# A spectral filter beside a routed expert layer on one core: the forward 32-point step of four pairs of groups on float16 halves, the last tile in column halves with some output transfers on ScalarE's queue, and a new order of the work

## The chip, the cores and the metric

One Trainium2 chip, one core. The core has a matrix engine (TensorE, PE in the profile), VectorE (DVE), ScalarE (ACT), GpSimd (POOL) and SyncE (SP), which issues the transfers; 16 DMA engines move the data. PE writes to PSUM, eight banks of 2 KB per partition; VectorE and ScalarE read it from there. The metric is device microseconds of one execution, the median over runs.

## The reference

Input `x` is 2048 by 576 (rows n, columns d). The result is the sum of two branches, each fed with the layer norm of `x`, and of `x` itself.

```python
X = rfft2(LN(x));  y_A = irfft2(X * (w_r + 1j * w_i), s=(2048, 576))      # spectral filter

q = einsum("nd,dhc->nhc", LN(x), w_q)          # 32 heads, c = 2 x 128
s1 = q[..., :128] @ k1.T;  s2 = q[..., 128:] @ k2.T      # 8 scores each
# top 1 of s1 and of s2 per head -> one of 64 experts; weights by softmax over K = 1
y_B = sum over heads of gelu(LN(x) . u[expert]) * v[expert]               # routed experts

out = x + y_A + y_B
```

The two-dimensional transform is written as matrix products: over d (576 points, folded by symmetry into even and odd halves) and over n (2048 = 64 x 32 points, with the filter's weights between the forward and the inverse half).

## The kernel before

**Forward, first half.** `x` lies in SBUF as 16 tiles of 128 rows (`XN`). Five loads bring it, of 2, 2, 4, 4 and 4 tiles (`LOADS`). For each tile `ln` finds mean and variance (on VectorE, for tiles 7, 9, 11, 13, 15 on ScalarE), `folds` makes sums and differences of mirrored columns (tiles `t` for the first fold, `F` in the tag `A2` for the second; `DF` lists the tiles whose odd part is folded on VectorE, the others go to GpSimd), ScalarE makes `Rs` (a 128-by-128 float32 matrix scaled by the rows' inverse deviations) and `yl` (three copies of the 33 columns left over), and `dft128` multiplies them on PE and stores the result in `AB` and `ABL`.

**The weights of the scores.** `fold_part` reads `w_q` once, in 32 transfers of 576 KB into five buffers `w`, and multiplies each with `KP` (the differences of the keys). `fold_end` and `fold_last` turn and scale the result (`MT`) into `MU` and `MUL`, in float16 high and low parts. With that the layer norm, the queries and the keys are one product of `x` with `MU`.

**The 16 groups of frequencies.** For a group g, `d_fwd(g)` is the step over d (PE, from `ABL` and `AB`, 6 matmuls; ScalarE copies the PSUM to a float32 tile `A2`). `s_fwd(g)` is the 32-point step of the pair g, g+1: 16 float32 matmuls on quarters of the array (64 by 64), weights `S16`, data `A2`. `s_mul(g)` multiplies by the filter's weights (two VectorE instructions of 578 columns, then GpSimd and ScalarE make `y`, `yh`, `yl`). `s_inv(g)` is the step back over n, 36 float16 matmuls on high and low halves (ScalarE and VectorE store the results in `AB`, `ABL`). `load_w` and `load_s16` fetch the weights ahead.

**The routed experts, r = 0 to 7**, 256 rows each. `x_t(r)` loads the transposed x (`xf`) and splits it into float16 halves (`xT`). `scores(r)` is 28 matmuls `MU,xT` and `MUL,xT` of 128 by 512, followed on VectorE by a reduce to `mx` and two products; `route` and `combine` are more VectorE work, with a few instructions on ScalarE, GpSimd and PE, and end in `CAT`.

**The end.** For tile t, `d_inv(t)` is the step back over d, with VectorE and GpSimd joining the halves; `fin(t)` multiplies the last 64-point step and the experts' part into PSUM (the matmuls `A,c` and `vS,MT`), VectorE adds `x` into `XN` (one instruction of 576 columns), and two transfers of 64 partitions by 288 columns by 2 rows (144 KB) go to the output. All are issued by SP.

**What sets the order.** Nothing is issued where it is written: every operation is recorded in a planner (`_Plan`) with an estimated cost and its dependences; a list scheduler (`forward`) then picks, engine by engine, the ready operation with the smallest number in a table, `RANK`, one number per operation; buffers (tags with 2 to 5 copies, as `w` 5 and `A2` 2 for groups and 4 for folds) and PSUM banks (`LIMIT`) hold operations back. The result is one fixed order per engine, and in it each engine issues strictly in turn. All operations are issued from one helper line, L542 of before, which is why the profile's rows all carry that line and are told apart by the tiles they name.

Of the kernel before, what the change touches and what calls it, by code (L numbers as in the profile page):

```python
# [32 lines left out]
def _consts():  # L33
# [55 lines left out]
    s16 = np.concatenate([(fw * 64).astype(np.float32), np.concatenate(_hl(iv), 2).view(np.float32)], 2)  # L89
# [42 lines left out]

CHANGE = 97.0

RANK = (
# [158 lines left out]
class _Plan:  # L294
# [7 lines left out]
    def cost(self, eng, m, out, ins, kw):  # L302
        n = 1
# [5 lines left out]
        if eng == "tensor":  # L309
# [5 lines left out]
            if kw.get("tile_position"):  # L315
                q = _parts(ins[0])
                return c * q[0] * q[1] / 16384 * (0.935 if q == [64, 128] else 1.065), 230.0
# [243 lines left out]
def _body(ctx, tc, nc, plan, a, out):  # L561
# [580 lines left out]
    def fin(t, y):  # L1142
# [12 lines left out]
        for c in range(2):  # L1155
            Q.dma_start(os[t, c], x[64 * c:64 * c + 64])
# [121 lines left out]
```

## Time and profile before

| what | value |
|---|---|
| median of three runs | 214.45 us (214.44 to 216.28) |
| the profiled execution, its own time | 215.94 us |
| its span, first to last instruction | 214.2 us |
| mean granted clock of TensorE | 0.987 |
| PE busy | 191.7 us (89%), 2324 matmul records |
| VectorE busy | 178.3 us (83%), 426 instructions |
| ScalarE, GpSimd busy | 129.8 us (61%), 112.9 us (53%) |
| moved by DMA | 48.12 MB, 225 GB/s over the span |

The page cuts the span into 40 slices of 5.36 us. In it PE is busy from the third slice to the last but one; VectorE is full at the start and from the nineteenth slice on, with a thinner middle; the DMA engines are full to the nineteenth slice, nearly idle in the stage of the experts, and half busy in the last six slices. A float32 matmul leaves several records in the trace, a float16 one leaves one. Times in the rows are microseconds from the start of the span: start, then duration; in square brackets stands how long the engine had been idle and what ended that.

### The profile page before, as it was taken

The page shows a single profiled execution, that of the slowest core. Times are in us where ns is not written, and L with a number is a line of the kernel's source. Part 1 is how long each engine was busy: PE and PEld are TensorE (multiplying, and loading weights), DVE is VectorE, ACT ScalarE, POOL GpSimd, SP SyncE. Part 2 cuts the span into 40 slices and gives each one's busy share as a digit, 9 for nine tenths or more (in the row PEclk, how much of TensorE's full clock was granted, in tenths as well). Part 3 has the DMA queues.
Part 4 walks back from the last instruction along what each step waited for, and adds up shares of the span by engine and source line. Part 5 has one row for each costly group of instructions (what it writes and reads, how often), then busy time and mean ns, then how long its engine had stood idle before and what let it go on. Part 6 is the DMA issues. An engine that isn't in the chain of part 4 may idle for free.

```text
span 214.2 us, 6027 instructions
## 1 busy us (share of the span) xinstructions
PE 191.7 (89%) x2324; PEld 131.4 (61%) x2324; DVE 178.3 (83%) x426; ACT 129.8 (61%) x304; POOL 112.9 (53%) x153
## 2 busy tenths in 40 slices
PE   0093999989999999999999999999999999999980
PEld 0082877757856765674648464476465777878850
DVE  1999899941694956992999999999999999999880
ACT  2279699888948792984845964996454531222310
POOL 4356464612419840492523663879565147758750
PEclk9999799999999999999999999999999999999998
DMA  6999999999999999998543433102000000655566
GB/s 202 392 413 422 396 312 313 415 409 410 384 384 387 411 410 381 424 411 352 142 123 95 153 112 95 55 3 77 0 5 0 3 0 5 167 139 139 123 161 164
DMA packets 17020, 48.12 MB, mean 225 GB/s; under 512 B 2144, under 2 KB 8544, under 8 KB 16224
## 3 DMA queue, kind: packets, MB, share of 16 engines
q1 hardware_dynamic: 16992, 47.74, 62.7%
q8 instruction: 18, 0.29, 0.6%
q14 instruction: 10, 0.08, 0.1%
HBM read 43.01 MB, written 4.72 MB: 223 GB/s over the span
## 4 chain that ended last, share of the span: by engine, by line
PE 54%; DVE 32%; issue 5%; ACT 2%; POOL 2%; DMA 2%; DVEq 0%; POOLq 0%
PE banks L542 54%; DVE t L542 8%; DVE MT L542 5%; DVE A L542 4%; DVE st L542 3%; DVE w L542 2%; DVE AB L542 2%; DMA XN<-in_x_dram 2%; DVE ABL L542 2%; POOL t L542 2%; DVE mx L542 1%; DVE mm__96 L542 1%; DVE rr L542 1%; ACT yl L542 1%; POOL y L542 1%
## 5 line engine op out<-in xcount | busy, mean ns | idle before, releaser
L542 PE MATMUL banks<-MU,xT 128*128 128x512 f16 x192 | 45.2, 379 | 0.0
L542 PE MATMUL banks<-c,AB 128*128 128x145 f16 (+2 forms) x320 | 37.7, 251 | 0.4 <-DVE AB L542 0.4
L542 PEld LDWEIGHTS <-xT 128*128 128x128 f16 x224 | 20.9, 98 | 23.7 <-issue 0.4
L542 POOL TENSOR_TENSOR y<-t,t 128x289 f32<-128x289 f32 x32 | 23.2, 744 | 21.3 <-DVE t L542 19.1
L542 POOL TENSOR_TENSOR A<-t 128x289 f32<-128x289 f32 (+2 forms) x42 | 26.5, 649 | 14.7 <-PE banks L542 5.6
L542 DVE SCALAR_TENSOR_TENSOR t<-banks,wx,Wt 128x578 f32<-128x578 f32 x32 | 24.4, 811 | 4.4 <-ACT A L542 2.8
L542 POOL TENSOR_TENSOR yh<-y,yh 128x578 f16<-128x578 f32 x16 | 20.8, 1309 | 10.2 <-ACT yh L542 6.8
L542 PE MATMUL banks<-Rs,yl 128*99 128x128 f32 x64 | 11.2, 319 | 15.0 <-ACT yl L542 14.7
L542 POOL TENSOR_TENSOR xT<-xf,xT 128x640 f16<-128x640 f32 x10 | 14.2, 1428 | 17.8 <-ACT xf L542 11.0
L542 ACT ACTIVATE AB<-banks 128x512 f32<-128x512 f32 (+1 forms) x32 | 18.7, 591 | 3.8 <-PE banks L542 3.7
L542 PE MATMUL banks<-w,KP 128*32 128x288 f32 x256 | 20.3, 415 | 0.2 <-DMA w<-in_wq_dram 0.2
L542 ACT ACTIVATE yh<-banks 128x290 f32<-128x290 f32 (+1 forms) x16 | 7.3, 458 | 20.2 <-PE banks L542 13.5
L542 PEld LDWEIGHTS banks<-Rs,yl 128*99 128x99 f32 x64 | 9.0, 195 | 16.7 <-ACT yl L542 15.1
L542 PE MATMUL banks<-c,ABL 99*128 99x289 f16 (+1 forms) x64 | 19.1, 298 | 0.0
L542 POOL TENSOR_TENSOR t<-XN 128x289 f32<-128x289 f32 x14 | 13.1, 942 | 10.9 <-DVE A L542 5.3
L542 PEld LDWEIGHTS banks<-c,AB 128*128 128x128 f32 x128 | 18.0, 190 | 1.3 <-DVE AB L542 0.6
L542 PEld LDWEIGHTS banks<-Rs,A 128*128 128x128 f32 x128 | 16.7, 207 | 3.3 <-issue 2.3
L542 PE MATMUL banks<-Rs,A 128*128 128x128 f32 x128 | 18.3, 295 | 0.0
L542 DVE TENSOR_REDUCE MT<-w 128x128 bf16<-128x896 bf16 (+1 forms) x16 | 18.2, 1138 | 0.0
L542 PE MATMUL banks<-A,s 64*64 64x289 f32 x256 | 17.5, 410 | 0.0
L542 PEld LDWEIGHTS <-AB 128*128 128x128 f16 x192 | 17.2, 147 | 0.1
L542 DVE TENSOR_TENSOR ABL<-banks,ABL 33x256 f16<-33x256 f32 x32 | 13.0, 410 | 5.0 <-ACT ABL L542 4.7
(129 smaller groups left out, 408.4 us busy)
## 6 DMA issues: line engine op xcount, KB each, us to landing
w<-in_wq_dram SPq DMA_DIRECT2D x32, 576.0 KB, 6.9
xf<-in_xT_dram SPq DMA_DIRECT2D x16, 320.0 KB, 5.1
Wt<-in_W_dram SPq DMA_DIRECT2D x8, 578.0 KB, 6.6
out_dram<-XN SPq DMA_DIRECT2D x32, 144.0 KB, 2.5
XN<-in_x_dram SPq DMA_DIRECT2D x3, 1154.0 KB, 9.2
s<-in_s_dram SPq DMA_DIRECT2D x16, 192.0 KB, 4.4
XN<-in_xd_dram SPq DMA_DIRECT2D x2, 1152.0 KB, 9.0
XN<-in_xd_dram SPq DMA_DIRECT2D x1, 2304.0 KB, 10.6
```

The costliest lines, as they stand in the source:

```text
L542: ins = fn(*[x.place() if isinstance(x, _Ps) else x for x in args], **{k: x.place() if isinstance(x, _Ps) else x for k, x in kw.items()}).ins
```

## The change

1. **`s_fwd` on float16 halves** for the groups 0 to 7 (`PAIRS = (0,1,2,3)`). The host gives the forward weights of these groups as high and low float16 halves, in the same bytes. In `d_fwd`, ScalarE writes the high half of `A2` as float16, and a new VectorE instruction subtracts it from the PSUM to make the low half (128 by 578), one for each of the 8 groups. `s_fwd` sums three products (high by high, low weight by high, high weight by low): 48 float16 matmuls for a pair in place of 16 float32 ones.
2. **The first load** of two tiles of `x` becomes two of one tile; `ln` treats these tiles one by one.
3. **`folds`**: in the tiles of `DF` the two VectorE additions of 145 columns become one of 2 by 145.
4. **`fin(15)`** in two column halves (columns 0 to 143 and 144 to 287 of each block): twice the matmuls at half the columns, two VectorE additions of 2 by 144, four transfers of 72 KB. The second transfer (`c` = 1) of tiles 13 and 14 and of both halves of 15 is issued from ScalarE's queue.
5. **The planner's constants** (costs of a few kinds of operation, the price of a change of matmul shape, a cold start of PE, the port that VectorE and GpSimd share) are altered, and `RANK` is new. The order of everything is made anew.

```diff
+PAIRS = (0,1,2,3,)
 RANK = (
-    464, 1220, 901, 1223, 1261, 1268, 1219, 1221, 391, 444, 431, 691, 894, 879, 874, 922, 835, 890, 883, 839,
...
+    1031, 1229, 1032, 1219, 1241, 1243, 1242, 1033, 1245, 730, 572, 810, 562, 803, 319, 320, 329, 377, 707,
...
-    s16 = np.concatenate([(fw * 64).astype(np.float32), np.concatenate(_hl(iv), 2).view(np.float32)], 2)
+    fw = np.stack([np.concatenate(_hl(v), 1).view(np.float32) if g // 2 in PAIRS else v.astype(np.float32) for g, v in enumerate(fw * 64)])
+    s16 = np.concatenate([fw, np.concatenate(_hl(iv), 2).view(np.float32)], 2)
...
-    LOADS = ((0, 2), (2, 2), (4, 4), (8, 4), (12, 4))
-    Q.dma_start(XN[:, 0:2], xs[:, 0:2])
+    LOADS = ((0, 1), (1, 1), (2, 2), (4, 4), (8, 4), (12, 4))
+    Q.dma_start(XN[:, 0:1], xs[:, 0:1])
...
-        (V if t in DF else G).tensor_tensor(F[:, 1, 0:145], e[:, 1, 0:145], e[:, 1, 288:143:-1], op=OP.add)
-        V.tensor_tensor(F[:, 0, 0:145], e[:, 0, 0:145], e[:, 0, 288:143:-1], op=OP.add)
+        if t in DF:
+            V.tensor_tensor(F[:, :, 0:145], e[:, :, 0:145], e[:, :, 288:143:-1], op=OP.add)
+        else:
+            G.tensor_tensor(F[:, 1, 0:145], e[:, 1, 0:145], e[:, 1, 288:143:-1], op=OP.add)
+            V.tensor_tensor(F[:, 0, 0:145], e[:, 0, 0:145], e[:, 0, 288:143:-1], op=OP.add)
...
     def d_fwd(g):
-        A2[g] = T([128, 2, L], F32, "A2", 2)
-        A.activation(A2[g], p[:, :, :L], AF.Copy)
+        if g // 2 in PAIRS:
+            A2[g] = T([128, 2, 2, L], F16, "A2", 2)
+            A.activation(A2[g][:, 0], p[:, :, :L], AF.Copy)
+            V.tensor_tensor(A2[g][:, 1], p[:, :, :L], A2[g][:, 0], op=OP.subtract)
+        else:
+            A2[g] = T([128, 1, 2, L], F32, "A2", 2)
+            A.activation(A2[g][:, 0], p[:, :, :L], AF.Copy)
...
     def s_fwd(g):
+        sf = [(S16[g + q][:, :192].bitcast(F16) if g // 2 in PAIRS else S16[g + q][:, :192]) for q in range(2)]
+        hl = ((0, 0), (0, 1), (1, 0)) if g // 2 in PAIRS else ((0, 0),)
         for m in range(2):
             for b in range(2):
-                w = 64 * (0, 1, 1, 2)[2 * m + b]
...
+                for n, (ha, hb) in enumerate(hl):
+                    w = 64 * (0, 1, 1, 2)[2 * m + b] + 192 * hb
...
+                            P.matmul(ps[q][o:o + 64, m, :L], sf[q][r, w:w + 64], A2[g + q][r, ha, b, :],
+                                     start=(b == n == 0), stop=(b == 1 and n == len(hl) - 1), tile_position=(64 * e, o))
...
     def fin(t, y):
+        x = XD[:, t]
+        if t == 15:
+            for n, z in enumerate((slice(0, 144), slice(144, 288))):
+                p = PS("bc"[n])
...
+                V.scalar_tensor_tensor(x[:, :, z], p[:, :, z], sc[:, 11:12], x[:, :, z], op0=OP.mult, op1=OP.add)
+                for c in range(2):
+                    (A if c else Q).dma_start(os[t, c, :, :, z], x[64 * c:64 * c + 64, :, z])
+            return
...
         for c in range(2):
-            Q.dma_start(os[t, c], x[64 * c:64 * c + 64])
+            (A if c and t > 12 else Q).dma_start(os[t, c], x[64 * c:64 * c + 64])
```

**Where the order changes, the loads.** On SP, at the start of the program (XN is x, w the 576 KB pieces of `w_q`, xf the transposed x of the scores, s the weights S16, c the constants), before:

```order
L542 DMA XN<-in_x_dram 128x1154 x2
L542 DMA kT<-in_kT_dram 128x16
L542 DMA c_68<-in_c_dram 128x320
L542 DMA mk<-in_mk_dram 128x99
L542 DMA s_3_118<-in_s_dram 128x384
L542 DMA XN<-in_x_dram 128x2308 x2
L542 DMA w_123<-in_wq_dram 128x1152
L542 DMA w_119<-in_wq_dram 128x1152
L542 DMA w_122<-in_wq_dram 128x1152
L542 DMA w_120<-in_wq_dram 128x1152
L542 DMA XN<-in_x_dram 128x2308
L542 DMA w_121<-in_wq_dram 128x1152
```

and at the same place of the changed kernel:

```order
L546 DMA XN<-in_x_dram 128x577 x2
L546 DMA kT<-in_kT_dram 128x16
L546 DMA s_2_117<-in_s_dram 128x384
L546 DMA XN<-in_x_dram 128x1154
L546 DMA c_68<-in_c_dram 128x320
L546 DMA XN<-in_x_dram 128x2308 x3
L546 DMA w_120<-in_wq_dram 128x1152
L546 DMA mk<-in_mk_dram 128x99
L546 DMA xf_124<-in_xT_dram 128x640
L546 DMA xf_125<-in_xT_dram 128x640
L546 DMA w_121<-in_wq_dram 128x1152
L546 DMA w_119<-in_wq_dram 128x1152
```

All of `x` now stands ahead of the first w; the constants `c` stand behind 192 KB of s and one more piece of x, and two pieces of xf come among the first w.

**Ahead of the first scores.** On PE, the last rows before the first matmul `MU,xT` (the matmuls `c,ABL` and `c,AB` are `d_fwd`, those of `A` and `s` are `s_fwd`), before:

```order
L542 LDWEIGHTS ABL
L542 MATMUL banks<-c_72,ABL 128x289
L542 MATMUL banks<-c_72,AB 128x145
L542 MATMUL banks<-c_72,AB 128x144
L542 LDWEIGHTS ABL
L542 MATMUL banks<-c_72,ABL 128x289
L542 MATMUL banks<-c_72,AB 128x144
L542 MATMUL banks<-c_72,AB 128x145
L542 LDWEIGHTS xT_94
L542 MATMUL banks<-MU,xT_94 128x512
```

and in the changed kernel:

```order
L546 LDWEIGHTS s_2_117
L546 MATMUL banks<-A_2_102,s_2_117 64x289
L546 LDWEIGHTS s_3_118
L546 MATMUL banks<-A_3_103,s_3_118 64x289
L546 LDWEIGHTS ABL
L546 MATMUL banks<-c_72,ABL 128x289
L546 MATMUL banks<-c_72,AB 128x145
L546 MATMUL banks<-c_72,AB 128x144
L546 LDWEIGHTS ABL
L546 MATMUL banks<-c_72,ABL 128x289
L546 LDWEIGHTS xT_94
L546 MATMUL banks<-MU,xT_94 128x512
```

In all, 72 matmuls of `d_fwd` (12 groups) stand ahead of the first scores before, and 64 in the changed kernel. The four `s_fwd` of the changed pairs, four `s_inv` and all 128 matmuls on w stand ahead of them in both.

**The last transfers.** On ScalarE, the end of the program before:

```order
L542 ACTIVATE CZ<-MT 128x2x64
L542 ACTIVATE MT<-banks 128x256
L542 ACTIVATE yh_134<-banks 128x290
L542 ACTIVATE MT<-banks 128x256
L1274 UNCONDITIONAL_BRANCH
```

and in the changed kernel:

```order
L546 ACTIVATE CZ<-MT 128x2x64
L546 ACTIVATE MT<-banks 128x256
L546 ACTIVATE yh_134<-banks 128x290
L546 ACTIVATE MT<-banks 128x256
L546 DMA out_dram<-XN 128x1x288 x2
L546 DMA out_dram<-XN 128x1x144 x2
L1304 UNCONDITIONAL_BRANCH
```

SP's last row was 32 such transfers of 288 columns; it is now 28, and two of 144. The four on ScalarE stand behind all its other work.

More of the change, by code (lines that the diff above doesn't have):

```diff
@@ L316, in cost @@
                 q = _parts(ins[0])
-                return c * q[0] * q[1] / 16384 * (0.935 if q == [64, 128] else 1.065), 230.0
+                return c * q[0] * q[1] / 16384 * (0.935 if q == [64, 128] else 1.037), 230.0
             return c, 230.0
+        if m == "dma_start":
+            return 450.0, self.land
         if eng == "scalar":
@@ L342, in add @@
         c += self.extra
-        if AF.Gelu_apprx_tanh in args and not self.asked:
+        if AF.Gelu_apprx_tanh in args and not self.asked and not self.extra:
             self.asked, c = True, c + 1283.0
@@ L473, in forward @@
                 if shape is not None and o.shape[0] != shape:
-                    t0 = max(t0, free[e] + CHANGE)
+                    t0 = max(t0, free[e] + (120.0 if o.shape[0] == [128, 128] else 90.0))
                 shape = o.shape[1]
-                if t0 - free[e] > 2500.0:
+                if t0 - free[e] > 2500.0 or not warm:
                     warm = t0 + (4500.0 if warm else 6000.0)
```

25 lines of the change are left out of this document (15 added, 10 removed), and 125 rows, old and new, of the table RANK.

## The prediction

> **What bounds the kernel now.** I read the waits of PE first, since the page gives it 89% of the span, then its timeline, then a table of busy times by stage, then the chain.
>
> ```profile
> PE banks L542 <- ACT yl L542: 14.7, 3, 10.9
> PE banks L542 <- DVE t L542: 0.9, 2, 0.5
> PE banks L542 <- DMA w<-in_wq_dram: 0.2, 1, 0.2
> ```
>
> PE waits in three places for `yl`, 14.7 us, 10.9 of it before its first matmul, and for hardly anything else. Its timeline shows the start and what a pause costs:
>
> ```profile
> 10.92 2.03 PE L542 MATMUL banks<-Rs,yl 128*99 128x128 f32 x8 [10.92 <-ACT yl L542]
> 12.74 2.60 PE L542 MATMUL banks<-Rs,A 128*128 128x128 f32 x16
> ...
> 21.16 2.03 PE L542 MATMUL banks<-Rs,yl 128*99 128x128 f32 x8 [3.10 <-ACT yl L542]
> 22.98 2.60 PE L542 MATMUL banks<-Rs,A 128*128 128x128 f32 x16
> ...
> 33.15 1.12 PE L542 MATMUL banks<-Rs,yl 128*99 128x128 f32 x8 [0.18 <-ACT Rs L542]
> 34.10 1.95 PE L542 MATMUL banks<-Rs,A 128*128 128x128 f32 x16
> ```
>
> The same 8 and 16 records cost 2.03 and 2.60 us after the waits of 10.92 and 3.10, and 1.12 and 1.95 us later: 1.56 us lost each time. By stage (PE, weight loads, VectorE, ScalarE, GpSimd, then clock, DMA share, GB/s):
>
> ```profile
> 45.00:55.00 10.00, 10.00 (x97) 7.67 (x98) 3.71 (x9) 9.20 (x19) 2.61 (x2) 1.00 1.01 403
> 55.00:65.00 10.00, 10.00 (x116) 6.78 (x116) 7.67 (x25) 6.38 (x13) 2.64 (x3) 1.00 1.02 390
> 65.00:75.00 10.00, 10.00 (x170) 6.34 (x172) 6.94 (x13) 8.66 (x16) 9.06 (x11) 1.00 1.01 396
> 75.00:85.00 10.00, 9.62 (x159) 6.21 (x160) 5.91 (x16) 5.77 (x14) 2.53 (x2) 1.00 1.03 397
> 85.00:95.00 10.00, 9.49 (x99) 6.97 (x98) 9.49 (x23) 8.92 (x19) 5.98 (x7) 1.00 1.02 415
> 95.00:101.90 6.90, 6.90 (x40) 3.36 (x39) 2.74 (x6) 3.44 (x7) 2.63 (x4) 1.00 0.89 360
> 101.90:144.00 42.10, 42.10 (x468) 25.15 (x472) 41.43 (x74) 30.72 (x65) 22.99 (x23) 1.00 0.34 98
> 144.00:178.40 34.40, 34.09 (x456) 21.70 (x445) 34.18 (x70) 17.20 (x47) 19.43 (x27) 1.00 0.05 13
> 178.40:209.10 30.70, 29.64 (x493) 23.64 (x493) 28.66 (x55) 7.61 (x22) 21.75 (x33) 1.00 0.54 130
> ```
>
> The reader is to see two regimes. From 45 to 101.9 us PE is full (55.99 of 56.9), the DMA engines are full to 95, and VectorE works 36.46 of 56.9, so it has 20.4 us idle. From 101.9 on PE and VectorE are both full: VectorE 104.3 of 107.2. The border is the first reduce of the routing:
>
> ```profile
> 101.94 1.09 DVE L542 TENSOR_REDUCE mx<-banks 128x128 f32<-128x896 f32 x1 [1.10 <-PE banks L542]
> ...
> 206.45 2.59 DVE L542 SCALAR_TENSOR_TENSOR XN<-banks,sc,XN 128x576 f32<-128x576 f32 x3 [0.25 <-PE banks L542]
> ```
>
> So VectorE's last addition ends at 209.04, 107.1 us after the first `mx`; the rest, 5.1 us to the span's end, is the output's tail. The profiled execution is 215.94 for a span of 214.2; the median, 214.45, is 1.49 below it. I work out differences from the trace and take them off the median.
>
> **The change part by part.**
>
> *f16 halves in the forward step.* What a pair costs, and what small float16 matmuls cost on the same quarters of the array:
>
> ```profile
> 60.25 2.18 PE L542 MATMUL banks<-A,s 64*64 64x289 f32 x32
> 62.37 1.18 PE L542 MATMUL banks<-w,KP 128*32 128x288 f32 x16
> ...
> 206.22 0.67 PE L542 MATMUL banks<-A,c 64*64 64x288 f32 x8
> 206.71 0.55 PE L542 MATMUL banks<-vS,MT 64*64 64x288 f16 x12
> 207.08 0.66 PE L542 MATMUL banks<-A,c 64*64 64x288 f32 x8
> ```
>
> A pair takes 62.37 − 60.25 = 2.12 us. Twelve float16 matmuls of the same shape, start to next start, take 0.37 us, 31 ns each; 48 take 1.49 us. Saved: 0.63 us for a pair, 2.4 us rounded down for four, all in the stage where PE is full.
>
> The eight new VectorE subtractions (128 by 578 from PSUM to float16) are not in the trace; the nearest rows are
>
> ```profile
> L542 DVE SCALAR_TENSOR_TENSOR t<-banks,wx,Wt 128x578 f32<-128x578 f32 x32 | 24.4, 811 | 4.4 <-ACT A L542 2.8 <-issue 1.1 <-PE banks L542 0.5
> L542 DVE TENSOR_TENSOR AB<-banks,AB 128x512 f16<-128x512 f32 x16 | 10.8, 677 | 2.2 <-ACT AB L542 2.2
> ```
>
> 677 ns for 512 columns makes some 740 for 578; 811 is the upper end. Eight are 5.9 us (at most 6.5). All stand ahead of the first `mx` in the new order, where the 20.4 idle us cover them: I cost them at 0. Each also lengthens the way from `d_fwd` to `s_fwd` by 0.74 us, covered as long as PE has matmuls on w or other groups to go on with, and behind a late one PE's whole queue stands. Without cover it is the third rival.
>
> *The order ahead of the scores.* 64 `d_fwd` matmuls instead of 72 stand before them, 1.3 groups less. The timeline's end of that stage:
>
> ```profile
> 85.26 1.18 PE L542 MATMUL banks<-w,KP 128*32 128x288 f32 x16
> ...
> 93.07 0.30 PE L542 MATMUL banks<-c,ABL 99*128 99x289 f16 x1
> ...
> 94.32 0.29 PE L542 MATMUL banks<-c,ABL 99*128 99x289 f16 x1
> ...
> 95.56 2.75 PE L542 MATMUL banks<-MU,xT 128*128 128x512 f16 x12
> ```
> ```profile
> 92.84 0.34 DVE L542 SCALAR_TENSOR_TENSOR MUL<-banks,sc,MUL 64x112 f16<-64x112 f32 x1
> ```
>
> A group costs 94.32 − 93.07 = 1.25 us, so PE could reach the scores 1.7 us sooner for that, but the work is only moved behind them, where PE is full too: 0 for the end while PE binds, up to −1.7 if VectorE alone does. I take 0. The loads set a floor: the DMA engines are full until 95, and the last w is used at 85.26 to 86.4. Ahead of it the new order has one more load of x in its second form (1152 KB) and one `Wt` (578) and one `xf` (320) less: 254 KB at 415 GB/s, 0.6 us later. From the last w to the scores before are 95.56 − 86.44 = 9.1 us; PE has only some 5.6 us of other work there now, so it may wait 1 to 2 us for `MU`. I enter +0.5 us for this and the longer `fin(15)` together (0 to 2.5).
>
> *The start.* First load and first statistics:
>
> ```profile
> 0.72 3.85 DMA XN<-in_x_dram
> 4.59 1.54 DVE st L542 x4
> ...
> L542 SPq DMA_DIRECT2D out_dram<-XN x32: 528/604/1879, 180.8 to 210.7; - x32
> ...
> DMA to landing us min/median/max: 2.4/2.5/4.3
> ```
>
> 577 KB land after 3.85 us, 144 KB at the least after 2.4; in a line between, 288.5 KB take 2.9, 0.95 sooner. One tile's statistics instead of two is another 0.77, and PE starts from some 9.2 instead of 10.92. Against it, the constants come behind 192 KB more, and the w's behind the last 8 tiles of x, so PE may have less to fill the later gap of 3.10 with. What survives lies between 0 and 2.4 (both gains and part of the second pause); I take 1.5. The merged additions of 2 by 145 save VectorE a few tenths, inside that range.
>
> *The tail.* SP issues the last transfers one every 604 ns (row above). DMA share by microsecond:
>
> ```profile
> 207.00:208.00 1.00, 1.00 (x30) 0.59 (x20) 0.97 (x2) 0.00 (x0) 0.00 (x0) 1.00 0.57 131
> 208.00:209.00 1.00, 0.11 (x4) 0.00 (x0) 0.90 (x2) 0.00 (x0) 0.00 (x0) 1.00 0.91 221
> 209.00:210.00 1.00, 0.00 (x0) 0.00 (x0) 0.04 (x1) 0.00 (x0) 0.00 (x0) 1.00 0.95 225
> 210.00:211.00 1.00, 0.00 (x0) 0.00 (x0) 0.00 (x0) 0.00 (x0) 0.00 (x0) 1.00 0.96 234
> 211.00:212.00 1.00, 0.00 (x0) 0.00 (x0) 0.00 (x0) 0.00 (x0) 0.00 (x0) 1.00 0.90 211
> 212.00:213.00 1.00, 0.00 (x0) 0.00 (x0) 0.00 (x0) 0.00 (x0) 0.00 (x0) 0.53 0.68 166
> ```
>
> By the issues alone, two queues would end four issues, 2.4 us, sooner, less the 0.8 us that the last addition holds them: about 1.5. But the engines are busy 4.97 of these 6 us. Only the 1.03 idle can be won, less what the smaller pieces of tile 15 cost. I take 0.7 (−0.3, if the pieces cost more than they win, to 1.0). The last addition comes in two halves, the first of which frees its transfers sooner; that is inside it.
>
> The Trainium skill, "DMA: Bandwidth & Descriptors", section "Issuing engines are not separate DMA queues", says that transfers started by different engines run interleaved on the same 16 DMA engines, so that a second issuer saves only issue time. The shares of 0.90 to 0.96 agree with it; taken strictly the tail wins nothing and the sum would be 0.7 us higher, while a reading by issue times alone would make it 0.8 lower.
>
> *Sum:* −2.4 (forward step) − 1.5 (start) − 0.7 (tail) + 0.5 (waits for `MU`, last tile) = −4.1: 214.45 − 4.1 = 210.35, say **210.3 us**. By the other way: first `mx` at 101.94 − 3.4 = 98.5, plus 107.1, plus a tail of 5.1 − 0.7, plus 1.74 around the span, is 211.7 against 215.94, the same but for rounding.
>
> **The rivals.**
>
> 1. *The tail is bound by the DMA engines and the small pieces eat the idle share*: tail gain 0, 211.0. For it speak the shares; against it the 0.57 in 207 to 208. It is also a faster outcome, inside the range.
> 2. *The last w and `MU` set the first `mx`.* DMA is full to 95 whatever PE does, VectorE (9.49 of 10 busy from 85 to 95) gets new work there, and PE arrives early only to wait. The last part of `MU` is ready at 93.18, 2.4 us before the scores, and the last w comes 0.6 later; with one subtraction of 0.74 in that chain the first `mx` moves by 2.4 − 0.6 − 0.7 = 1.1 only, whatever PE saves. With 0.7 in the tail that is 212.6 us: no change. Against it: PE waited 0.2 us for w in all, so the loads have slack before.
> 3. *Slower: the low halves are not covered.* VectorE issues in order; its 20.4 idle us are partly waits that nothing can fill (in 85 to 95 only 0.51 idle). If the eight subtractions all come in front of work that PE waits for, the first `mx` moves by their 5.9 us, and the forward step's 2.4 is lost in PE's waits: 214.45 + 5.9 − 1.5 − 0.7 = 218.2. It decides once PE waits more than 0.63 us for each low-half pair; it ends slower than before from a loss of 1.2 us a pair on. Against it: from 45 to 85 VectorE is busy 26.97 of 40.
> 4. *Float16 matmuls on quarters don't stream at 31 ns in this pattern* (here each has its own weights to load). At 44 ns, the price at which 48 cost the old 2.12, the term vanishes: 212.7 us. Against it, the weight loads take 6.2 to 7.7 of each 10 us from 45 to 95, so they have room.
>
> **How the numbers follow.** The forecast and rival 1 are one side: 0.70 together (0.52 and 0.18). Rival 2 has 0.12, rival 4 has 0.06, rival 3 has 0.12. About 1% is what a measurement of this kernel can tell from no change, 2.1 us: faster means under 212.3, slower over 216.6. Faster takes the 0.70 and little of the others: 0.71; within 1%: 0.17; slower: 0.12. The low end: start 2.4 instead of 1.5, tail 1.0, no wait, and 0.8 of the moved groups: 210.3 − 0.9 − 0.3 − 0.5 − 0.8 = 207.8, say 207.5. The high end takes in rivals 2 and 4 and stops short of rival 3: 214.0.
>
> **What the changed profile would show.** Forward step right: the rows of `A,s` come as 48 float16 records in about 1.5 us, with no wait of PE for `A` over 0.6. Start right: PE's first matmul at 9 to 9.6, waits for `yl` 1.5 us shorter in sum. First `mx` at 97.5 to 99.5, the last addition 107 later. Tail right: the last landing under 4.6 us after the last addition, DMA share over 0.9 throughout. The prediction is wrong if PE's waits list `A`, w or `MU` with several microseconds, or if VectorE's work after `mx` grew.

## The result, and the profile of the changed kernel

The changed kernel took 213.19 us in the median of 8 runs (212.53 to 213.36); the kernel before, run beside it, 215.99 us (214.34 to 216.28). The ratio is 0.9888, with a 95% interval of 0.9855 to 0.9922: faster by 1.1%, where 1.9% was forecast. Three of the eight runs of before lie near 214.4 us, the forecast's base, and five near 216; against 214.45 the gain is 1.3 us where 4.1 was forecast, and a later section finds what parts the two levels. The profiled execution took 213.16 us, its span is 211.4, against 215.94 and 214.2.

The waits of PE in the changed kernel (engine, what it did, what it waited for; us in total, times, longest) answer to those shown of before:

```profile
PE banks L546 <- ACT Rs L546: 11.2, 4, 9.5
PE banks L546 <- ACT yl L546: 1.8, 2, 1.3
PE banks L546 <- DMA w<-in_wq_dram: 0.3, 1, 0.3
```

PE now waits 13.0 us for `Rs` and `yl` (14.7 for `yl` before), and the pause of 3.10 us is gone; the longest after the first is 1.3. Its timeline at the start and at one of the float16 steps:

```profile
9.54 2.03 PE L546 MATMUL banks<-Rs,yl 128*99 128x128 f32 x8 [9.54 <-ACT Rs L546]
11.36 3.62 PE L546 MATMUL banks<-Rs,A 128*128 128x128 f32 x16
15.94 0.68 PE L546 MATMUL banks<-Rs,yl 128*99 128x128 f32 x4 [0.96 <-ACT Rs L546]
...
64.28 1.68 PE L546 MATMUL banks<-A,s 64*64 64x289 f16 x48
65.89 0.30 PE L546 MATMUL banks<-c,ABL 99*128 99x289 f16 x1
```

PE starts 1.38 us sooner, and a pair of groups takes 65.89 − 64.28 = 1.61 us instead of 2.12. The span falls into three stretches, divided by the first `mx` and by the end of VectorE's last addition into `XN`. The table of busy times (columns as in the prediction) for the second and third stretch, the kernel before first:

```profile
101.94:209.04 107.10, 105.78 (x1410) 70.45 (x1406) 104.27 (x197) 55.53 (x132) 64.17 (x83) 1.00 0.30 80
209.04:214.17 5.13, 0.00 (x0) 0.00 (x0) 0.00 (x0) 0.00 (x0) 0.00 (x0) 0.80 0.67 161
```

and the changed kernel:

```profile
45.00:96.57 51.57, 50.85 (x693) 34.53 (x690) 39.27 (x90) 38.41 (x78) 25.61 (x26) 1.00 1.02 411
96.57:205.88 109.31, 107.36 (x1446) 71.73 (x1444) 105.69 (x201) 57.31 (x136) 63.77 (x83) 1.00 0.31 85
205.88:211.37 5.49, 0.00 (x0) 0.00 (x0) 0.00 (x0) 0.00 (x0) 0.00 (x0) 0.84 0.54 152
```

| stretch | before | changed | difference | forecast |
|---|---|---|---|---|
| start to first `mx` | 101.94 | 96.57 | −5.37 | −3.4 |
| first `mx` to last addition | 107.10 | 109.31 | +2.21 | 0 |
| last addition to end of span (the tail) | 5.13 | 5.49 | +0.36 | −0.7 |
| span | 214.17 | 211.37 | −2.80 | −4.1 |

Against this trace of before, 2.0 us more was won ahead of the first `mx` than forecast, all of that surplus was given back behind it, and the tail, which was to be shorter, got longer. The experiments go through these in turn; 1.5 of the 5.37 us turn out to belong to this one trace of before and not to the change.

In each experiment, the numbers that order the work were replaced by the positions in the order of the kernel that it starts from, and each engine keeps that order strictly, so that nothing moves but what is said. The traces bear that out: with the output on one queue, which touches the tail alone, the first `mx` comes at 96.48 and the stretch behind it takes 109.32 us, as in the changed kernel.

### The profile page after: what moved, and what is told of

It is laid out like the page before. It is cut to its first block, busy times and chain, and to the rows that moved or that the text cites. A ratio compares the mean times of both kernels' runs of the same rounds, so it can differ in the third digit from the quotient of the medians.

```text
span 211.4 us, 6192 instructions
## 1 busy us (share of the span) xinstructions
PE 189.9 (90%) x2408; PEld 130.6 (62%) x2408; DVE 183.6 (87%) x430; ACT 129.9 (61%) x305; POOL 110.4 (52%) x153
## 4 chain that ended last, share of the span: by engine, by line
PE 61%; DVE 28%; issue 3%; ACT 2%; DMA 2%; POOL 1%; DVEq 0%; POOLq 0%
PE banks L546 61%; DVE t L546 6%; DVE MT L546 4%; DVE st L546 4%; DVE A L546 3%; DVE w L546 2%; DVE AB L546 2%; DMA XN<-in_x_dram 2%; DVE ABL L546 1%; DVE rr L546 1%; DVE mx L546 1%; DVE mm__96 L546 1%; DVE mv L546 1%; DVE mxr L546 1%; DVE al L546 1%
## 5 line engine op out<-in xcount | busy, mean ns | idle before, releaser
L546 POOL TENSOR_TENSOR y<-t,t 128x289 f32<-128x289 f32 x32 | 23.8, 766 | 18.4 <-DVE t L546 12.8
L546 POOL TENSOR_TENSOR A<-t 128x287 f32<-128x287 f32 (+2 forms) x42 | 26.2, 641 | 8.8 <-DVE t L546 4.7
L546 PEld LDWEIGHTS banks<-Rs,yl 128*99 128x99 f32 x64 | 8.3, 180 | 16.5 <-ACT Rs L546 11.9
L546 POOL TENSOR_TENSOR t<-XN 128x289 f32<-128x289 f32 x14 | 11.5, 824 | 11.4 <-DVE rr L546 3.2
L546 ACT ACTIVATE A<-banks 128x578 f16<-128x578 f32 (+1 forms) x16 | 10.4, 650 | 8.8 <-PE banks L546 8.8
L546 PE MATMUL banks<-A,s 64*64 64x289 f16 (+1 forms) x320 | 15.6, 336 | 0.0
```

The source lines that it names most:

```text
L546: ins = fn(*[x.place() if isinstance(x, _Ps) else x for x in args], **{k: x.place() if isinstance(x, _Ps) else x for k, x in kw.items()}).ins
```

## Experiments

### Which part won what ahead of the first `mx`

**The forward step in float32 again.**

```diff
-PAIRS = (0,1,2,3,)
+PAIRS = ()
```

> The changed kernel with all forward 32-point steps in float32 again: the eight VectorE subtractions are gone, every other instruction stands in the changed kernel's order. Theory P (PE is full from the first w to the end, the subtractions lie in VectorE's idle time): the four pairs in the changed kernel's trace take 1.6 us each against 2.12 before, so this one is 2.0 us slower than the changed kernel (ratio to before about 0.998), and its first mx comes 2.0 later than 96.6. Rival S (the subtractions cost what the matmuls save): no difference, ratio 0.989. Rival V (VectorE alone sets the time, so its 5.9 us count): faster than the changed kernel by some us.

Measured: 214.67 us (ratio 0.9961, 0.9926 to 0.9996), 1.5 us above the changed kernel. The trace tells the parts:

```profile
98.90 1.09 DVE L552 TENSOR_REDUCE mx<-banks 128x128 f32<-128x896 f32 x1 [1.07 <-PE banks L552]
...
205.71 2.52 DVE L552 SCALAR_TENSOR_TENSOR XN<-banks,sc,XN 128x576 f32<-128x576 f32 x4 [0.25 <-PE banks L552]
```

The first `mx` comes 2.33 us later than 96.57 and the last addition, which ends at 208.23, 2.35 later than 205.88: theory P holds, the float16 step is worth 2.3 us, and the eight subtractions (749 ns each in the changed kernel's groups) cost nothing that shows. The time is only 1.5 above, because the tail of this kernel is 4.42 us and not 5.49; the reason is the subject of the tail's experiments.

**The first load in one piece again.**

```diff
-    LOADS = ((0, 1), (1, 1), (2, 2), (4, 4), (8, 4), (12, 4))
-    Q.dma_start(XN[:, 0:1], xs[:, 0:1])
+    LOADS = ((0, 2), (2, 2), (4, 4), (8, 4), (12, 4))
+    Q.dma_start(XN[:, 0:2], xs[:, 0:2])
...
-    for t, n in ((0, 1), (1, 1), (2, 2), (4, 4), (8, 4), (12, 4)):
+    for t, n in ((0, 2), (2, 2), (4, 4), (8, 4), (12, 4)):
```

> The changed kernel with the first load of x as one transfer of two tiles again and the square root of the two tiles in one, the rest in the changed kernel's order. Theory P (the earlier start is carried to the end): PE's first matmul at 10.9 instead of 9.54, the end 1.4 us later, ratio 0.995. Rival E (the earlier start is given back in the waits for Rs and yl that follow: 0.96, 1.33, 0.26, 0.51, 0.42 us): these waits shrink, first mx within 0.3 us of 96.6, ratio 0.989.

Measured: 215.23 us (ratio 0.9976, 0.9947 to 1.0006). PE starts at 10.74, the first `mx` comes at 98.18 and the last addition ends at 207.53, 1.65 us after the changed kernel's. The waits for `Rs` and `yl` behind the start do not shrink (1.9 and 2.2 us behind the first one, against 1.7 and 1.8 in the changed kernel). Theory P holds: what the start wins is carried to the end, and it is 1.65 us by the traces (2.0 by the medians, of runs from 214.38 to 216.98).

Start and forward step together are 4.0 of the 5.37 us. One would like to put the other 1.4 down to the 1.3 groups of `d_fwd` that the new order moves behind the first scores (1.7 us by the prediction's row), but another cause covers it. In a trace of the old order without the loss of clock that the section on the two traces of before explains (two queues on the kernel before), the first `mx` comes 1.46 us sooner than in the trace used so far:

```profile
100.48 1.09 DVE L548 TENSOR_REDUCE mx<-banks 128x128 f32<-128x896 f32 x1 [1.10 <-PE banks L548]
```

From there to 96.57 are 3.9 us, and start and forward step (1.61 and 2.33 at the first `mx`) are all of it. So no gain from the moved groups is shown; no run undid that move alone.

### What sets the stretch behind the first `mx`

The prediction entered the moved groups at 0, since PE looked full on both sides of the border. Two kernels change PE's work behind it, in opposite ways for VectorE.

```diff
-                for ha, hb in ((0, 0), (0, 1), (5, 0)):
+                for ha, hb in (((0, 0), (0, 1), (5, 0)) if r == 0 or c < 3 else ((0, 0), (0, 1))):
                     P.matmul(p[:, i, :], xt[:, ha + c, :], MU[:, hb, c, :], start=(n == 0), stop=False)
```

> The changed kernel without 14 of the scores' matmuls (the low half of x by the high half of MU for the fourth block of columns, in r = 1 to 7), all of which stand behind the first mx: 3.0 us of PE work less in that stage, nothing else altered. In the changed kernel from the first mx to the last addition are 109.3 us (before: 107.1), with VectorE busy 105.7 and PE 107.4 or so. Theory V (VectorE sets the length of that stage): 109.3 stays within 0.5. Theory P (PE is full, work moved there counts): 106.3 to 106.8.

```diff
-PAIRS = (0,1,2,3,)
+PAIRS = (0,1,2,3,4,5,6,7,)
```

> The changed kernel with float16 halves for all eight pairs: behind the first mx VectorE has eight subtractions more (0.74 us each, 5.9) and PE four pairs at 1.6 instead of 2.12 us (2.0 less). Theory V: from the first mx to the last addition 113 to 115.5 us instead of 109.3. Theory P: 107.3 to 108.5. Both at work: 109 to 112.

Measured: 213.88 us (ratio 0.9896, 0.9824 to 0.9969) and 218.90 us (1.0129, 1.0045 to 1.0212). The stretch from the first `mx` to the last addition, first without the 14 matmuls, then with all pairs in float16:

```profile
96.73:206.95 110.22, 105.03 (x1432) 70.62 (x1430) 107.00 (x201) 56.93 (x136) 63.76 (x83) 1.00 0.30 84
```

```profile
97.70:211.93 114.23, 107.85 (x1510) 72.84 (x1508) 110.99 (x207) 57.56 (x136) 64.78 (x83) 1.00 0.29 80
```

With 2.3 us less of PE's busy time the stretch is not shorter but 0.9 longer; with eight more VectorE instructions it is 4.9 longer, although PE was to do 2.0 less. VectorE's busy time follows in both (107.00 and 110.99 against 105.69). So theory P falls, and V's reading holds: behind the first `mx` VectorE sets the length, and PE's 98% busy doesn't bind it. V's own number for the first kernel, 109.3 within 0.5, was missed by 0.4; where the 1.3 us more of VectorE come from is said below.

That the stretch grew by 2.21 us is then a matter of VectorE: it is busy 1.4 us longer (105.69 against 104.27) and idle 0.8 longer. One of the two largest pieces is a product of 128 by 16 elements, `al`. VectorE in the changed kernel, and GpSimd at the same time:

```profile
151.98 1.26 DVE L546 TENSOR_TENSOR al<-wx,mk 128x16 f32<-128x16 f32 x1
```

```profile
151.90 1.31 POOL L546 TENSOR_TENSOR yh<-y,yh 128x578 f16<-128x578 f32 x1 [0.48 <-DVE mx L546]
```

Before, the same product took 0.17 us (at 152.95, with GpSimd's `yh` starting 0.5 us later). It now starts 0.08 us after the long GpSimd instruction and ends with it. The Trainium skill ("SBUF — State Buffer", section "SBUF: two separate sides") says that the two engines share a pair of ports under an exclusive lock, so that, for an instruction of VectorE with two inputs in SBUF like this one, the later of them waits for the whole of the other's instruction; the two rows, which end at 153.24 and 153.21, agree. The other piece stands at 127.60, where VectorE's 128 by 64 takes 1.43 us instead of 0.21 beside a GpSimd instruction that runs from 127.39 to 128.95. Together they lose 2.3 us. Before, the three longest losses beside GpSimd were some 0.5 each, 1.5 in all (at 105.49, 188.83 and 195.83), so such meetings make about half of the 1.4.

They also account for the kernel with fewer matmuls. There `al` and the 128 by 64 take their short times, but three products of 128 by 128 meet GpSimd (1.39, 1.37 and 1.33 us instead of 0.28, at 122.03, 126.40 and 128.69) and one of 128 by 512 loses 0.4 (at 142.19): 3.7 us in all, 1.3 more than the two lose in the changed kernel, which is the 1.3 that VectorE is busy longer. The first of them, on VectorE and on GpSimd:

```profile
122.03 1.39 DVE L552 TENSOR_TENSOR MT<-MT 128x128 f32<-128x128 int32 x1
```

```profile
121.87 1.40 POOL L552 TENSOR_TENSOR xT<-xf,xT 128x640 f16<-128x640 f32 x1 [0.78 <-ACT xf L552]
```

To see what such a meeting costs the kernel, `al` went to GpSimd (together with the 64 small matmuls at the start that the next part explains):

```diff
-        V.tensor_tensor(al, wx[:, 0, :], gm, op=OP.mult)
+        G.tensor_tensor(al, wx[:, 0, :], gm, op=OP.mult)
```

> The changed kernel with the 64 one-column matmuls at the start, and the small product al (128 by 16) on GpSimd instead of VectorE. In the changed kernel al takes 1.26 us on VectorE and ends with GpSimd's yh of 1.31 us; before it took 0.17. Theory V (VectorE sets the stage from the first mx to the last addition, and loses 1.1 us there to GpSimd): 108.0 to 108.5 us from the first mx to the last addition instead of 109.3, and a time of 211.0 against 212.06 with the 64 matmuls alone. Rival G (the loss moves to the next VectorE instruction or is idle time anyway): 109.0 to 109.4, 212.0.

Measured: 211.15 us (210.91 to 212.81; ratio 0.9803, 0.9746 to 0.9860). From the first `mx` to the last addition:

```profile
96.67 1.09 DVE L552 TENSOR_REDUCE mx<-banks 128x128 f32<-128x896 f32 x1 [0.88 <-PE banks L552]
...
202.48 2.52 DVE L552 SCALAR_TENSOR_TENSOR XN<-banks,sc,XN 128x576 f32<-128x576 f32 x4 [0.25 <-PE banks L552]
```

205.00 − 96.67 = 108.3 us, 1.0 less than 109.3, and the time is 0.9 below that of the same kernel without this edit. VectorE is busy 104.64 us there, 1.05 less than in the changed kernel: what it saved in this stretch, the kernel saved. This is the fastest kernel of the study.

### The tail

**One queue, and tile 15 whole.** First the two parts of the tail's change were undone one at a time.

```diff
-                    (A if c else Q).dma_start(os[t, c, :, :, z], x[64 * c:64 * c + 64, :, z])
+                    Q.dma_start(os[t, c, :, :, z], x[64 * c:64 * c + 64, :, z])
...
-            (A if c and t > 12 else Q).dma_start(os[t, c], x[64 * c:64 * c + 64])
+            Q.dma_start(os[t, c], x[64 * c:64 * c + 64])
```

> The changed kernel with all output transfers on SP's queue; tile 15 still in column halves. In the changed kernel from the end of the last VectorE addition to the end of the span are 5.5 us, before 5.1. Theory D (the DMA engines bind the tail, who issues does not matter): 5.3 to 6.2, within 0.7 us of the changed kernel. Rival Q (two queues disturb each other): 5.1 or less, faster than the changed kernel by 0.4 or more. Rival I (one read of 16 KB of instructions, 1.38 us on one DMA engine at 205.2, holds every transfer of that moment, since each uses all 16 engines): the transfers issued around 204 to 206 still land 4 us after their issue, as in the changed kernel, and the tail stays at 5.3 to 6.5.

```diff
-        if t == 15:
+        if t == 99:
```

> The changed kernel with tile 15 whole (one VectorE addition of 576 columns, two transfers of 144 KB), its second transfer and those of tiles 13 and 14 on ScalarE's queue. Theory D: the same bytes in larger packets, tail 0 to 0.4 us shorter or longer than the 5.5 of the changed kernel, the last addition within 0.3 us of 205.9. Rival H (small pieces cost): tail shorter by over 0.5 us. Rival I (read of instructions): transfers issued around 204 to 206 still take 4 us, SP and ScalarE are held in issuing for over 1 us.

Measured: 214.83 us on one queue (ratio 0.9947, 0.9918 to 0.9975) and 212.73 us with tile 15 whole (0.9849, 0.9802 to 0.9896). With the last addition where it was (205.80 and 206.24), the tail is 7.57 us on one queue, and 4.41 with tile 15 whole. So two queues help, by 2.1 us in this order (1.6 by the medians), more than any theory had said, since none had put the tail on one queue over 6.5; rival Q falls. Something costs 1.1 us (0.5 by the medians) when tile 15 comes in halves, which spoke for rival H. But the trace shows one more thing. In the changed kernel, two single issues among the last transfers, one by SP and one by ScalarE:

```profile
205.07 1.90 SPq L546 DMA_DIRECT2D out_dram<-XN  x1
```

```profile
205.74 1.24 ACTq L546 DMA_DIRECT2D out_dram<-XN  x1
```

They take 1.90 and 1.24 us instead of the usual 0.6, and both end at about 206.97. The DMA queues of the changed kernel from 204.5 to 207 us (packets, MB, share of 16 engines):

```profile
q1 hardware_dynamic: 390, 0.40, 62.2%
q10 hardware_dynamic: 205, 0.22, 31.2%
q8 instruction: 1, 0.02, 3.5%
...
out_dram<-XN ACTq DMA_DIRECT2D x2, 144.0 KB, 4.0
out_dram<-XN SPq DMA_DIRECT2D x2, 144.0 KB, 4.3
```

One packet of the kind "instruction", 16,384 bytes from 205.18 on, holds one of the 16 DMA engines for 1.38 us (3.5% of 16 engines in 2.5 us), and the transfers of that time land after 4.0 to 4.3 us instead of 2.5. Such reads come every 7 to 10 us in this part of both kernels; the last one of before stood at 205.3, ahead of all but two of the last ten transfers. With tile 15 whole PE has 16 matmuls less, and the read does not come until 211.8, after the last landing. That is a second difference between the two kernels, and so tile 15 whole does not tell small pieces (H) from the read (I).

**Moving the read.** Small matmuls on a zeroed tile, ahead of PE's first, while it waits for x, add instructions to PE's stream and shift its reads:

```diff
+    pw_ = PS("m", (128, 512))
+    for k in range(64):
+        P.matmul(pw_[:, 0:1], CZ[:, 0:128], CZ[:, 0:1], start=True, stop=True)
```

once 64 of them, with tile 15 in halves, and once 24, with tile 15 whole.

> The changed kernel as it is, with 64 such one-column matmuls at the start: 128 instructions more, 256 make one read of 16 KB, PE goes through about 33 a microsecond at the end. The read at 205.2 should come at about 201.3, ahead of the last four tiles' transfers. Theory I: tail of 4.0 to 4.5 us instead of 5.5, the kernel 1.0 to 1.4 us faster than the changed one. Rival H (small pieces): tail 5.3 or more, no gain. Rival Q (two queues on the same engines): tail 5.3 or more.

> The changed kernel with tile 15 whole, and 24 matmuls of one column on a zeroed tile ahead of PE's first, in the time in which PE waits for x anyway; nothing reads their results. They are 48 instructions more, so that PE's reads of 16 KB of instructions come earlier in the program: the read that stood at 211.8, after the last landing, with tile 15 whole (and at 205.2 in the changed kernel) should come at about 204 to 205, among the last transfers. Theory I (that read is what makes the changed kernel's tail long): from the last addition to the span's end 5.3 to 5.7 us instead of 4.4, transfers around the read land after about 4 us instead of 2.4 to 3.4, the kernel 1.0 us slower than with tile 15 whole alone. Rival H (it is the small pieces of tile 15): tail stays at 4.4, same time as with tile 15 whole.

Measured: 212.06 us with the 64 (211.88 to 212.12; ratio 0.9813, 0.9758 to 0.9869), 1.1 us below the changed kernel. The read stands at 201.6, and from 204.5 to 207 us the DMA queues show none:

```profile
q1 hardware_dynamic: 374, 0.38, 57.9%
q10 hardware_dynamic: 264, 0.28, 39.7%
...
out_dram<-XN ACTq DMA_DIRECT2D x2, 144.0 KB, 2.7
out_dram<-XN SPq DMA_DIRECT2D x2, 144.0 KB, 3.1
```

The tail is 4.37 us, with small pieces and two queues. Rivals H and Q fall; the read was the cost. Other kernels with tile 15 in halves and two queues agree: tails of 4.40 to 4.47 us where the read came ahead of the last ten transfers (float32 forward step, all pairs float16, the two with `al` on GpSimd), 5.32 and 4.95 where it fell among them, 0.7 us ahead of the last addition's end (one load of two tiles, fewer scores' matmuls).

The other half of the test did not come out as theory I said: with tile 15 whole and the 24 matmuls the median is 212.76 (212.20 to 215.03; ratio 0.9864, 0.9794 to 0.9935), no slower than without them, which is what rival H had said of this kernel. Its trace is of the run at 215.03, with a fall of the clock near the start. In it the read stands at 207.1, not at 204 to 205, the transfers around it land after 3.0 to 3.3 us, and the tail is 4.43. The read there took 0.88 us and came 1.7 us ahead of the end of the last addition; in the changed kernel it took 1.38 and came 0.7 us ahead. So a read among the last transfers need not cost anything; it did in the three traces with the halves on two queues. Its length alone does not decide that: in the kernel with fewer scores' matmuls the read took 0.88 us too, came 0.7 us ahead, and the tail was 4.95. Whether it is the place, the number of transfers that are waiting or the halves themselves, these runs leave open.

**Two queues on the kernel before.**

```diff
-            Q.dma_start(os[t, c], x[64 * c:64 * c + 64])
+            (A if c and t > 12 else Q).dma_start(os[t, c], x[64 * c:64 * c + 64])
```

> The kernel before with one thing altered: the second transfers of tiles 13, 14 and 15 are issued from ScalarE's queue; tile 15 is whole and the order is the old one, so the read of instructions at 205.3 stays ahead of the last six transfers but two. Theory I with the forecast's own term (two queues win 0.7 us in the tail, and only the read among the last transfers took that away): from the last addition to the span's end 4.3 to 4.5 us instead of 5.1, the kernel 0.7 us faster than before. Theory D (the DMA engines, 90 to 96% busy in the old tail, bind it): 4.9 to 5.2. Rival Q (two queues disturb each other): over 5.1.

Measured: 215.68 us against 216.19 (ratio 0.9972, 0.9940 to 1.0005), and a tail of 4.54 us instead of 5.13. The forecast's term for the second queue, 0.7 us, is right within about 0.1 where no read comes between; the ratio alone would not tell it from nothing.

### Why two traces of before and its median did not fit together

The prediction took its differences from an execution of 215.94 us off a median of 214.45. The times of the kernel before, over all its runs, lie near 214.4 to 214.8 or between 215.5 and 216.5, with one at 217.3. Another trace of it was taken:

> The kernel before once more, for its trace: its times fall near 214.4 and near 216.2. If this execution is one near 214.4, the stretches up to the first mx (101.9), from there to the last addition (107.1) and from there to the end (5.1) show which of them is 1.5 to 1.8 us shorter; if it is one near 216.2, all three agree with the old trace within 0.2.

It took 216.41 us, with the three stretches at 102.43, 107.10 and 5.11: the level near 216 again, so it did not show the other one. The trace of the kernel with two queues did, by luck: it took 213.93 us, with the same stretch behind the first `mx` (107.12), and the first `mx` at 100.48 (the row stands above). The clock granted from 21 to 25 us, in the trace of before, in the second trace, and in that one:

```profile
21.00:25.00 4.00, 3.84 (x21) 3.84 (x22) 3.19 (x14) 2.36 (x8) 1.83 (x2) 0.58 1.03 425
```

```profile
21.00:25.00 4.00, 3.70 (x20) 3.70 (x21) 3.19 (x14) 2.41 (x8) 1.98 (x2) 0.58 1.03 425
```

```profile
21.00:25.00 4.00, 3.74 (x36) 3.16 (x40) 4.00 (x16) 3.44 (x11) 1.38 (x3) 1.00 1.03 425
```

This is the time behind PE's second pause. The mean clock of the whole execution parts the levels, too: in the 26 runs of before beside these kernels it is 0.995 to 0.997 in the 9 runs up to 214.78 us, and 0.986 to 0.990 in the 17 from 215.60 on. At a clock of 0.58 PE got through 21 and 20 records, at full clock through 36. In the third trace the 16 records ahead of the pause had taken 3.62 us instead of 2.60, so that the pause, which ends at the same time, was 2.32 us and not 3.10. To test it, the pause was filled with 28 matmuls of 128 columns on the zeroed tile, on the kernel before.

> The kernel before with 28 matmuls of 128 columns on a zeroed tile in PE's second pause (18.1 to 21.2 us in its trace); nothing reads their results, all else in the old order. The times of the kernel before fall near 214.4 and near 216.2; in two traces near 216 the granted clock is 0.50 and then 0.65 to 0.67 from 21 to 25 us, behind this pause, in a trace at 213.9 (second queue in the tail) it is 1.00 there. Theory C (the two levels are that pause, after which the clock falls in some executions): with the pause filled the clock stays 1.00 from 21 to 25, all times lie within 0.5 us of 214.4. Rival N (the levels come from elsewhere): times on both levels as before, near 214.4 and 216.2.

Measured: 215.03 us (214.55 to 215.41, 10 runs; ratio 0.9979, 0.9952 to 1.0006). The clock is 1.00 from 21 to 25, and none of the ten runs is at 216, while 7 of the 13 runs of before beside it were above 215.5. That bears out theory C for the upper level. But the filled kernel's own level is 0.6 us above 214.4 and its range is wider than was said; the first `mx` of its trace, 101.37, is 0.9 later than 100.48, and the cause of that stays open.

### PE at work from the start

PE's first 24 records are slow as well (2.03 us for the first 8 in the changed kernel, 1.12 later in the program), though the clock granted from 9 to 13 us is 1.00 there. If that comes of standing still, PE kept busy until x arrives should gain them.

```diff
-        P.matmul(pw_[:, 0:1], CZ[:, 0:128], CZ[:, 0:1], start=True, stop=True)
+        P.matmul(pw_[:, 0:128], CZ[:, 0:128], CZ[:, 0:128], start=True, stop=True)
```

> As the kernel with al on GpSimd, but the 64 matmuls at the start have 128 columns, so that PE is at work until its first real matmul. Theory W (the first 24 real records lose 0.9 to 1.5 us because PE had stood still): the first eight records take 1.1 us instead of 2.0, PE is 0.5 to 1 us earlier at the first mx. Rival E (PE waits for Rs and yl anyway): first mx within 0.2 us, no gain.

Measured: 211.83 us (ratio 0.9843, 0.9767 to 0.9919), 0.7 us above the same kernel with one-column matmuls. Its PE:

```profile
9.57 1.12 PE L552 MATMUL banks<-Rs,yl 128*99 128x128 f32 x8 [2.36 <-ACT Rs L552]
10.52 1.95 PE L552 MATMUL banks<-Rs,A 128*128 128x128 f32 x16
15.97 1.17 PE L552 MATMUL banks<-Rs,yl 128*99 128x128 f32 x4 [3.50 <-ACT Rs L552]
16.94 1.91 PE L552 MATMUL banks<-Rs,A 128*128 128x128 f32 x8
```

The first 24 records run as fast as later ones, as theory W said, but the next ones are not fed sooner: PE now pauses 3.50 us instead of 0.94 and is slow behind that pause (1.17 and 1.91 us where 0.68 and 1.06 are usual; the clock from 13 to 21 us is 0.77 to 0.80). The first `mx` comes 0.7 us later. Both theories missed it: the gain turned into a pause that cost more.

## Why the prediction was right and wrong

**The forward step: right.** −2.4 forecast, 2.35 by the run without it. The time of a pair came out at 1.61 us against 1.49, so the price of 31 ns was a little low: by the rows four pairs save 2.0 us, the run shows 0.3 more, and the total agrees partly by luck. The subtractions (749 ns measured, 740 estimated) were hidden, as was said; the rivals of uncovered subtractions and of matmuls at 44 ns are out. VectorE's work from 45 to 85 us is 24.2 of 40 by the prediction's own table, not 26.97, which makes its case against uncovered subtractions stronger.

**The start: right.** −1.5 forecast, 1.65 by the run. PE's first matmul at 9.54 lies in the 9 to 9.6 that was named, through a first landing at 4.0 us, later than the 3.6 that the line between two sizes gave, and fewer VectorE instructions behind it.

**The stretch behind the first `mx`: this step failed.** "Plus 107.1" carried the old stretch over, and "I take 0" for the moved groups rested on PE being full behind the first `mx`. It isn't what binds there; VectorE is, and the forecast had no term for what the new order does to VectorE in that stretch. It took 109.31 us, 2.2 more: 1.4 us more busy and 0.8 more idle. Of the 1.4, about half come of its meetings with GpSimd; the rest is mostly three short instructions more and the second addition of `fin(15)`. The 0.8 idle no run explains. Nor did the prediction's other branch come true, up to −1.7 if VectorE alone binds: no gain of the moved groups shows ahead of the first `mx`. The prediction had named the sign, "if VectorE's work after `mx` grew", and it grew.

**Ahead of the first `mx`: right but for the waits.** Against the trace of before without the loss of clock, 3.9 us were won where 3.4 were forecast. The difference is the +0.5 entered mostly for PE's wait for `MU`, which did not come: PE's waits list 0.5 us for a scale and 0.3 for the loads, and rival 2 is out.

**The tail: this step failed.** "I take 0.7" became a loss of 0.36, an error of 1.1 us. The term itself was right where no read of instructions came between (4.37, 4.42, 4.54 against 5.13). The range for it, −0.3 to 1.0, knew nothing of that read, though the trace had it: two of the old kernel's output transfers, issued at 187.58 and 203.90, took 4.0 and 4.3 us to land, with a read of instructions at 188.92 and at 205.34, and the row with "2.4/2.5/4.3" showed the largest. I quoted this row and did not ask what the 4.3 was. The sign that I named for the tail could not show its failure: the last landing came 4.54 us after the last addition, under the 4.6 named, but before it had been 4.16; the DMA share, which was to stay over 0.9, fell to 0.52 from 207 to 208.

The reason given for 0.7 was wrong as well. I read a DMA share of 0.90 to 0.96 as the engines' limit at 211 to 234 GB/s. With two queues the share is hardly higher, but the rate is much. The kernel with tile 15 whole:

```profile
206.00:207.00 1.00, 0.00 (x0) 0.00 (x0) 0.24 (x1) 0.00 (x0) 0.00 (x0) 1.00 0.99 271
207.00:208.00 1.00, 0.00 (x0) 0.00 (x0) 0.00 (x0) 0.00 (x0) 0.00 (x0) 1.00 1.03 334
```

334 GB/s at a share of 1.03, from packets of the same 1152 bytes. The rule that I cited from the Trainium skill ("DMA: Bandwidth & Descriptors", section "Issuing engines are not separate DMA queues"), that a second issuer saves no more than issue time, is not borne out in this tail: the packets themselves went faster. Whether that comes of the second queue or of more transfers waiting at once, no run here separates. The rival built on it, tail gain 0, came nearest to the measured tail, for a different reason.

**The base: on another level than the trace.** The differences belonged to an execution at 215.94, and I took them off 214.45. The 1.5 us between the two are the clock behind the second pause. The changed kernel has no pause of that length, and its 8 runs lie within 0.9 us; so the level near 214.4 is the one to compare it with, and there the stretches add up: −3.9 ahead of the first `mx` (−3.4 forecast), +2.2 behind it (0) and +0.4 in the tail (−0.7) make −1.3, the difference between 214.45 and 213.19, where −4.1 was forecast. Against 215.94 the gain of 2.8 holds another 1.5 us that came with the pause, and no term of the sum named it: the 1.56 us that PE lost behind the pause of 3.10 were counted as a fixed cost of the kernel, when they were there in some of its executions only. One run at 215.03, in the kernel with 24 small matmuls, had a clock of 0.50 from 17 to 25 us, so the new order is not free of it. That 213.19 lies between the 207.5 and 214.0 named is luck: the upper end was set for rivals 2 and 4, and neither happened.

## What to carry to other kernels

Before adding differences up, ask for each stage which engine binds it: a PE that is 98% busy but comes second behind a VectorE in order gives nothing back when its work is cut, and a microsecond of VectorE that is saved there was one of the kernel here. Look in its rows for short instructions that take long beside one of GpSimd; a new order can make or lose such meetings. At the end of a program, look at when the transfers land and not at how busy the DMA engines are, and look for anything else on those engines. When a kernel's times fall on two levels, find out on which of them the profiled execution lies before taking its numbers off the median.

## What the runs showed of the hardware

- Reads of 16,384 bytes of instructions share the DMA engines with the data. In these traces one takes 0.88 to 1.76 us on one engine, and with a read of 1.38 us among them the last output transfers landed after 4.0 to 4.4 us instead of 2.4 to 2.5. Adding 128 instructions at the start of PE's stream, in its idle time, moved such a read from 205.2 to 201.6 us and made the kernel 1.1 us faster. The Trainium skill ("Runtime: NRT & Kernel Launch", section "Instruction fetch mechanics") says that instructions come in blocks of 16 KiB, 256 of them, and that the cost of crossing a block is mostly hidden; the size agrees with the trace; that page speaks of the engine's own cost, and what the read cost the last transfers was not hidden. With tile 15 whole a read of 0.88 us, 1.7 us ahead of the last addition's end, cost nothing.
- Output packets of 1152 bytes took about 77 ns while one queue was in use, and 54 to 59 while two had transfers waiting (tile 15 whole, and two queues on the kernel before); the rate went from 211 to 234 GB/s to as much as 334, at a DMA share of 0.90 to 0.96 and of 1.03. Whether the second queue or the number of transfers waiting does it, no run separates.
- An instruction of VectorE on 128 by 16 elements took 1.26 us instead of 0.17 when it started 0.08 us behind a GpSimd instruction of 1.31 us, and both ended together; given to GpSimd, it left the stretch 1.0 us shorter.
- Behind a pause of PE of 2.87 or 3.10 us the granted clock was 0.58 over 4 us, behind one of 2.32 at the same place 1.00 (2.03 us or 1.45 for the same 8 records). With the pause filled, none of ten runs was at the level near 216.
